# Loading the first MLP weight in four pieces of 512 columns instead of six, with the column blocks of chunk 0 reordered to match

## The chip, the cores and the metric

The kernel runs on one core of a Trainium2 chip. The metric is the device time of one execution in microseconds, the median over several runs; lower is better. Matrix products run on TensorE (PE in the profile; its weight loads are PEld), elementwise work on VectorE (DVE), ScalarE (ACT) and GpSimd (POOL); SyncE (SP) and GpSimd issue the transfers (DMA) that bring inputs from HBM to SBUF.

## What is computed

Linear attention over 8 batches of 8 heads (sequence 576, head size 64), and on its output, seen as 4608 tokens of 512 features, a two-layer MLP with a SiLU between:

```
q_s = softmax of q over the features of a head
k_s = softmax of k over the sequence
kv  = k_s^T v                       # 64 x 64 per head
x   = (q_s kv), heads side by side  # 4608 x 512
h   = x @ w_in                      # 512 -> 2048
out = silu(h) @ w_out               # 2048 -> 512
```

Inputs and output are float32; the kernel works in bfloat16 with float32 sums.

## The kernel before, in words

**Tiling.** The 4608 tokens are cut into 9 chunks of 512 (`NCH`, line 60). All that concerns chunk t and the attention of a later batch is interleaved in stage t by a plan written out by hand: `PLAN[t]` gives for each step a position in the stage, and lines 641 to 731 put all steps in one list, sort it by position and call them. Every engine then runs its own instructions in that order. `STEADY` is the plan of stages 3 to 7. The first product of chunks 0 and 1 and half of that of chunk 2 are plain, as is the second product of chunk 0; all others run by a scheme with seven products in place of eight.

**The start.** Batch 0 is loaded by SP (lines 558 to 562). GpSimd copies one element of v(0) into `gate` (line 583), so that its own loads begin only when the first half of v(0) is there, and then issues the loads of `WORDER` (line 28): the first four at line 584, the rest at line 635. The first weight `w_in`, 512 x 2048, becomes `W1` in bfloat16; `load_w` (line 567) brings it in six pieces: `w10` to `w13` of 256 columns each, `w14` and `w15` of 512. The number is the place in the columns; the order of loading is w11, w13, w10, w12, w14, w15. Behind them on the same queue stand q, k, v of batch 1 and the four pieces of the second weight (`w20` to `w23`, line 575). A float32 source and a bfloat16 destination: a piece of 256 columns writes 256 KB, one of 512 writes 512 KB.

**Chunk 0.** Its first product runs over 16 blocks of 128 columns of `w_in`, each in two halves: `part[0]` cuts the first 576 tokens into 320 and 256. `PLAN[0]['order']` lists the 32 block-halves (block, half). `mm1` (line 243) issues the four matmuls of one (line 251) into a PSUM buffer of a ring of six; `act1` (line 260) writes its silu from there into `GT` (line 281), for a 256-wide half in two instructions of 192 and 64, since chunk 0 ends inside it. The first two entries of the order are begun before the attention output `XT` is complete (line 632: the two quarters that are there, the others when the loop comes by). The second product of chunk 0 is `mm2` (line 523, matmuls at line 530).

**Around it.** In the same stage ScalarE takes the exponentials of batch 1 (line 114), between silus, each change with a table load; `vcast` copies v into `vaug` (lines 123 and 125); `kv` (line 171) multiplies k and v into `kvps` (line 178); `kvcopy` (line 186) scales that by the reciprocal of the sums into `kvn`, on VectorE (line 198) or ScalarE (line 196), as the plan's `ke` says for each half `cc`; `xt` (line 203) makes from it the next chunk's input (line 220). In stages 2 to 8 `product1` (line 319) and `sum1` (line 353) form the first product, `silu1` (line 379) its silu, `presum` (line 396) sums over `GT`, on the engine that `pbe` names, and `product` (line 422) the second product.

Of the kernel before, what the change touches and what calls it, by code (L numbers as in the profile page):

```python
# [9 lines left out]
BF16 = mybir.dt.bfloat16  # L10
# [2 lines left out]
AX = mybir.AxisListType  # L13


PLAN = {
    0: {'y': [31.0, 31.5, 33.5, 34.0, 34.0, 34.5, 35.0, 35.5, 36.0, 38.5, 40.0, 41.0, 42.0, 44.0, 45.5, 46.5], 'ex': [28.8, 28.3, 35.8, 30.3], 'qs': [38.0, 36.5], 'qn': [38.51, 38.01], 'vs': [31.5, 39.5], 'ks': [43.0, 40.5], 'kc': [46.01, 43.6], 'lq': 41.5, 'tp': 40.5, 'ox': [47.5, 47.5], 'oc': [47.51, 47.6], 've': [2, 1], 'order': [(3, 0), (2, 0), (0, 0), (0, 1), (3, 1), (5, 0), (6, 0), (4, 0), (2, 1), (1, 0), (7, 1), (1, 1), (11, 1), (8, 1), (6, 1), (12, 0), (11, 0), (14, 0), (10, 1), (4, 1), (12, 1), (7, 0), (8, 0), (5, 1), (13, 0), (10, 0), (9, 1), (13, 1), (15, 1), (9, 0), (15, 0), (14, 1)], 'ke': [1, 0], 'oe': [1, 1], 'qe': [1, 0], 'pad': 16},
    1: {'ex': [15.2, 17.22, 22.74, 19.26], 'qs': [18.0, 18.5], 'qn': [18.01, 19.1], 'vs': [24.0, 20.0], 'ks': [26.0, 22.0], 'kc': [27.01, 26.01], 'lq': 13.5, 'lk': 19.6, 'lv': 22.2, 'tp': 19.5, 'ox': [28.0, 28.0], 'oc': [28.51, 28.51], 've': [2, 2], 'pa': [10.9, 13.5, 14.0], 'pae': [0, 0, 0], 'ke': [0, 0], 'oe': [2, 0], 'std': 4, 'order': [], 'add': {}, 'act': {}, 's1': {0: 1, 1: 0, 2: 0, 3: 1}, 'sl': [2.5, 2.5, 2.0, 6.0, 4.5, 6.0, 6.0, 9.0, 8.0, 9.0, 10.5, 11.0, 12.5, 14.0, 15.0, 15.0], 'xs': [7.3, -20.9, 0.5, -6.5], 'xe': [0, 1, 1, 1], 'pad': 14, 'qe': [1, 0]},
    2: {'std': 2, 'order': [(3, 1), (3, 6), (2, 1), (2, 6), (3, 7), (3, 5), (2, 2), (2, 7), (3, 4), (3, 2), (2, 5), (2, 4), (2, 3), (3, 3)], 'y': [-12.5, -12.5, -11.5, -11.0, -11.0, -10.0, -10.0, -10.0, -9.0, -8.0, -5.5, -2.5, -2.0, -1.0], 'ex': [-1.207, -2.202, -0.08, 1.794], 'qs': [9.4, 3.4], 'qn': [11.41, 6.91], 'vs': [1.42, 11.4], 'ks': [19.4, 19.4], 'kc': [19.41, 19.41], 'lq': 19.95, 'lk': 14.762, 'lv': 26.91, 'tp': 12.9, 'ox': [19.9, 20.4], 'oc': [19.91, 20.91], 'sl': [4.5, 5.0, 2.5, 7.5, 5.0, 6.0, 10.0, 10.5], 'add': {(3, 6): 10.55, (3, 7): 12.55, (3, 3): 22.02, (3, 2): 16.02, (3, 1): 9.55, (3, 5): 13.55}, 'act': {(2, 3): 21.02, (3, 5): 17.02, (3, 3): 22.02, (2, 5): 18.55, (3, 4): 18.55, (2, 2): 18.02, (3, 1): 10.02, (2, 1): 11.55, (2, 6): 12.02, (3, 2): 17.55, (2, 4): 21.02}, 's1': {2: 0, 3: 1}, 'xs': [0.1, 1.1, 8.1, 8.1], 'pa': [19.45, 20.45, 20.95], 'ya': {5: -6.0, 3: 1.0, 4: -2.05}, 'm1': [0, 0], 'pb': [-14.4, -13.8, -13.9, -15.5, -9.5], 'xe': [0, 0, 0, 0], 'pae': [1, 1, 1], 'pbe': [0, 0, 0, 1, 0], 've': [1, 2], 'ke': [0, 1], 'oe': [1, 0], 'qe': [1, 0]},
}  # L20
STEADY = {'std': 0, 'order': [(0, 1), (0, 6), (0, 5), (0, 7), (0, 2), (1, 1), (0, 4), (1, 6), (0, 3), (2, 1), (1, 2), (1, 7), (1, 5), (2, 6), (1, 4), (1, 3), (2, 2), (2, 7), (2, 5), (2, 4), (3, 1), (3, 6), (2, 3), (3, 2), (3, 7), (3, 5), (3, 4), (3, 3)], 'y': [0.5, 1.5, 5.0, 6.0, 9.0, 9.5, 9.5, 12.5, 14.5, 18.0, 19.5, 22.5, 25.7, 28.402], 'ex': [3.798, 1.41, 3.92, 1.297], 'qs': [11.4, 6.9], 'qn': [12.41, 9.91], 'vs': [10.9, 12.92], 'ks': [19.4, 19.4], 'kc': [21.91, 20.41], 'lq': 8.95, 'lk': 23.9, 'lv': 24.41, 'tp': 17.4, 'ox': [23.4, 23.4], 'oc': [24.41, 26.41], 'sl': [], 'add': {(3, 6): 22.02, (0, 3): 8.02, (0, 2): 6.02, (0, 5): 5.02, (2, 2): 20.02, (1, 3): 15.55, (1, 4): 15.55, (2, 7): 17.55, (1, 2): 10.55, (0, 4): 8.02, (1, 1): 6.02, (2, 6): 14.55, (1, 6): 10.55, (3, 1): 20.55, (1, 7): 11.55, (3, 2): 24.02}, 'act': {(0, 2): 4.55, (0, 3): 10.02, (2, 5): 18.55, (0, 4): 9.02, (1, 5): 15.02, (3, 3): 27.404, (1, 3): 18.02, (0, 5): 5.02, (3, 4): 26.55, (1, 4): 17.02, (2, 4): 23.02, (2, 3): 23.02, (0, 6): 4.02, (1, 1): 8.02, (3, 6): 22.55, (0, 1): 2.55, (3, 5): 27.55, (2, 1): 13.02, (3, 2): 23.55, (3, 7): 27.02, (1, 7): 13.55, (2, 6): 15.02, (2, 7): 17.02, (1, 2): 12.55}, 's1': {0: 0, 1: 1, 2: 0, 3: 0}, 'xs': [0.296, 0.298, -0.227, 0.4], 'pa': [19.95, 27.407, 27.41], 'pb': [1.45, 1.96, 4.45, 5.46, 3.45], 'ya': {6: 8.0, 5: 18.5, 4: 22.95, 3: 28.852, 7: 14.5}, 'm1': [0, 0], 'xe': [0, 0, 1, 1], 'pae': [1, 1, 1], 'pbe': [0, 0, 1, 1, 1], 've': [1, 2], 'ke': [0, 1], 'oe': [0, 0], 'qe': [1, 1]}
for _t in range(3, 8):
    PLAN[_t] = STEADY
PLAN[8] = {'std': 0, 'order': [(0, 1), (0, 6), (0, 2), (0, 7), (1, 1), (0, 5), (0, 4), (0, 3), (1, 6), (1, 2), (1, 7), (1, 5), (1, 4), (2, 1), (1, 3), (2, 6), (2, 2), (2, 7), (2, 5), (3, 1), (2, 4), (2, 3), (3, 6), (3, 2), (3, 7), (3, 5), (3, 4), (3, 3)], 'y': [1.5, 2.0, 5.5, 8.5, 10.0, 11.0, 14.0, 15.0, 19.5, 22.0, 24.5, 25.8, 27.401, 27.406], 'sl': [], 'add': {(2, 7): 17.55, (3, 2): 24.02, (3, 7): 24.55, (3, 4): 26.55, (3, 1): 20.55, (2, 3): 22.55, (0, 2): 3.55, (0, 3): 8.02, (2, 4): 20.55, (1, 4): 14.02}, 'act': {(2, 1): 15.55, (3, 6): 24.02, (3, 4): 26.55, (2, 3): 24.55, (2, 4): 21.55, (1, 7): 14.02, (2, 6): 19.02, (0, 3): 10.02, (1, 5): 12.55, (0, 4): 8.02, (3, 5): 27.403, (1, 4): 15.02, (2, 7): 21.02, (3, 7): 25.55, (1, 6): 10.02, (1, 3): 15.55, (3, 2): 23.55, (2, 2): 19.02, (3, 1): 20.02, (0, 5): 7.55, (1, 1): 6.55}, 's1': {0: 1, 1: 0, 2: 1, 3: 1}, 'xs': [-0.71, -0.208, -0.207, 1.4], 'pa': [24.45, 27.45, 29.429], 'pb': [0.793, 3.96, 10.45, 8.46, 9.45], 'ya': {6: 10.0, 4: 27.401, 7: 15.45, 2: 11.95}, 'm1': [0, 0], 'xe': [0, 0, 1, 0], 'pae': [1, 1, 1], 'pbe': [0, 1, 0, 1, 0]}
PLAN[9] = {'y': [0, 1, 2, 3, 4, 5, 6, 7, 8, 9, 10, 11, 12, 13], 'ya': {}, 'm1': [0, 0], 'pb': [-0.201, -0.2, -0.2, 1.9, 2.9], 'pbe': [0, 0, 0, 0, 0]}
TXAT = [(0, (0, -10.0, 0, 0)), (0, (0, 16.0, 1, 0)), (1, (1, -24.5, 0, 1)), (1, (0, 20.5, 1, 0)), (2, (0, 25.5, 0, 1)), (2, (2, -28.0, 1, 0)), (3, (2, -25.0, 0, 0)), (3, (1, -12.5, 1, 0))]
TWAT = [(1, -7.0, 1), (0, 38.0, 0), (1, 3.5, 0), (0, 46.0, 0), (1, 9.5, 1), (1, 20.5, 0), (1, 10.0, 0), (0, 39.0, 0)]
WORDER = ['w11', 'w13', 'w10', 'w12', 'w14', 'w15', 'q', 'w21', 'w20', 'k', 'w22', 'v', 'w23']
GATE = ('vt', 0)
HV = (1, 0.0, 0)  # L30
JS = 5
STD = 0
START = {'qn': (0, 0), 'h': [3, 3, 2, 2], 'v': 0, 't': (0, 0, 0, 2), 'x': 1, 'o': 0, 'w': 4}

@with_exitstack
def kernel(
# [13 lines left out]
    nc = tc.nc  # L50
# [6 lines left out]
    NC = DM // 128  # L57
# [10 lines left out]
    glob = ctx.enter_context(tc.tile_pool(name="glob", bufs=1))  # L68
# [15 lines left out]
    warm = glob.tile([128, 512], BF16, name="warm")  # L84
    dummy = glob.tile([1, 1], FP32, name="dummy")
    gate = glob.tile([1, 8], FP32, name="gate")

    ld = ctx.enter_context(tc.tile_pool(name="ld", bufs=1))
    ap = ctx.enter_context(tc.tile_pool(name="ap", bufs=2))
# [5 lines left out]
    st = [dict() for _ in range(B)]  # L95
# [13 lines left out]
    def exp(b, src, dst, cc, js=(0, J)):  # L109
        if dst not in st[b]:  # L110
            st[b][dst] = ap.tile([128, J, NG * D], BF16, name=dst, bufs=1)
        js = slice(*js)
        o = st[b][dst][:, js, cc * 128:(cc + 1) * 128].rearrange("p j (g d) -> p j g d", d=D)
        nc.scalar.activation(out=o, in_=jgd(st[b][src], cc)[:, js], func=ACT.Exp)  # L114

    def vcast(b, cc, eng, gs=(0, 2)):
        if gs[0] == gs[1]:
            return
        gs = slice(2 * cc + gs[0], 2 * cc + gs[1])
        o = vaug.rearrange("p j (g e) -> p j g e", e=E1)[:, :, gs, 0:D]  # L120
        i = st[b]["vt"][:, gs, :].rearrange("p g (j d) -> p j g d", d=D)
        if eng is nc.scalar:
            eng.copy(out=o, in_=i)
        else:
            eng.tensor_copy(o, i)
# [167 lines left out]
    def xsum(t, i):  # L293
        V = ENG[PLAN[t]["xe"][i]]
        w = width(t)
# [57 lines left out]
    def sum1(t, g, k):  # L353
# [12 lines left out]
        if k == 1:  # L366
            if PLAN[t]["s1"][g]:
                nc.vector.tensor_scalar_mul(out=new("s1"), in0=o, scalar1=1.0)
# [182 lines left out]
    PSB = {"ring": 6, "ops": 2}  # L551


    nc.vector.memset(dummy, 0.0)
    nc.vector.memset(warm, 0.0)
    nc.scalar.activation(out=dummy, in_=dummy, func=ACT.Exp)
# [9 lines left out]

    def load_w(name):
        if name[:2] == "w1":
            f = slice(*((0, 256), (256, 512), (512, 768), (768, 1024), (1024, 1536), (1536, 2048))[int(name[2])])
            nc.gpsimd.dma_start(  # L570
                out=W1[:, :, f], in_=w_in[:, f].rearrange("(c p) f -> p c f", p=128)
            )
        elif name[:2] == "w2":
            i = int(name[2])
            nc.gpsimd.dma_start(
                out=W2[:, i * 4:(i + 1) * 4, :],
                in_=w_out[i * 512:(i + 1) * 512, :].rearrange("(fc p) o -> p fc o", p=128),
            )
        else:
            load(1, name + "t", {"q": q, "k": k, "v": v}[name], eng=nc.gpsimd)  # L580

    gx = st[0][GATE[0]]
    nc.gpsimd.tensor_copy(gate[:, 0:1], gx[0:1, 2 * GATE[1] + 1, 0:1])
    for name in WORDER[:START["w"]]:
        load_w(name)

    wps = ps.tile([128, 512], FP32, name="wps", tag="ops", bufs=PSB["ops"])

# [7 lines left out]
    for cc in range(2):  # L596
        exp(0, "qt", "eq", cc)
        qsum(0, cc)
        if cc == 0 or not SB["o"]:
            qnorm(0, cc, ENG[SB["qn"][cc]])  # L600
    exp(0, "kt", "ek", 0)
    vcast(0, 0, nc.scalar)
    exp(0, "kt", "ek", 1)
    for js in HALF:
# [77 lines left out]
    for t in range(NCH):  # L682
        p = PLAN[t]
# [4 lines left out]
        else:  # L688
# [4 lines left out]
            for i, (g, m) in enumerate(p["order"]):  # L693
                x = i + 4 * p["std"]
# [9 lines left out]
    for t in range(1, NCH):  # L704
        for i, (m, a) in enumerate(HALVES):
            x = PLAN[t + 1]["y"][i]
# [14 lines left out]
    for t in range(1, NCH):  # L721
# [5 lines left out]
        for i in range(5):  # L727
            n, h = ((0, 1), (1, 1), (2, 1), (3, 0), (3, 1))[i]
# [33 lines left out]
```

## Time and profile before

| | |
|---|---|
| median of 6 runs | 273.05 us (271.61 to 274.58) |
| the profiled execution | 272.63 us |
| span of its profile | 270.8 us |
| granted TensorE clock | 1.0 throughout |
| HBM read, written | 36.70 MB, 9.44 MB |

The profile is of one execution, and times in it count from the start of the span. Its page gives the busy time of each engine, the transfers, the chain of work that ended last, and groups of instructions; behind it stands the trace, which can be asked for the timeline of a stretch, for the waits of an engine, or for one line of the kernel. A group reads: line, engine, operation, tile written <- tile read, count. `W<-in_moe_w_in_dram` is a load of `w_in`, `hps` the PSUM tile of the first product, `ops` that of the second. The time of a load counts from its issue on GpSimd's queue to its landing.

### The profile page before, as it was taken

What the parts mean: (1) busy time and instruction counts of PE and PEld (TensorE: products, weight loads), DVE (VectorE), ACT (ScalarE), POOL (GpSimd) and SP (SyncE); (2) the same over time, 40 slices, a digit from 0 to 9 for tenths busy, and PEclk for the clock granted to TensorE, in tenths of its full rate; (3) what the DMA queues carried; (4) which work ended last, traced back from release to release, by engine and by line L of the source; (5) the groups of instructions that cost most, each with busy time, mean ns of one, the idle gap of its engine ahead of it and who ended that gap; (6) DMA issues with size and microseconds to landing.
All of it is one profiled execution on the core that took longest, in us unless ns stands there. A gap on an engine that the chain in (4) does not pass through costs nothing.

```text
span 270.8 us, 6537 instructions
## 1 busy us (share of the span) xinstructions
PE 254.2 (94%) x2668; PEld 198.5 (73%) x2668; DVE 199.6 (74%) x343; ACT 190.3 (70%) x317; POOL 145.0 (54%) x91
## 2 busy tenths in 40 slices
PE   8769999998998899999999999999999999999992
PEld 3437844456764778888888888887888887888882
DVE  2933476845968977978996899688978678898832
ACT  5678999578749897977987798769875457444300
POOL 1577126213302869794979397849685546604500
PEclk9999999999999999999999999999999999999999
DMA  7999998980797795579745965482531102110324
GB/s 255 307 164 292 273 317 157 363 315 0 222 289 257 95 346 187 192 139 309 238 127 119 325 238 117 102 306 94 119 84 45 40 21 59 41 39 18 78 65 116
DMA packets 44014, 46.50 MB, mean 172 GB/s; under 512 B 18640, under 2 KB 31952, under 8 KB 43984
## 3 DMA queue, kind: packets, MB, share of 16 engines
q1 hardware_dynamic: 37728, 38.22, 47.8%
q0 software_dynamic: 6096, 7.73, 13.4%
q8 instruction: 21, 0.34, 0.5%
q10 hardware_dynamic: 160, 0.13, 0.2%
q14 instruction: 9, 0.07, 0.1%
HBM read 36.70 MB, written 9.44 MB: 170 GB/s over the span
## 4 chain that ended last, share of the span: by engine, by line
PE 53%; DMA 14%; ACT 10%; DVE 10%; issue 5%; POOL 4%; SPq 2%; DVEq 0%; POOLq 0%; ACTq 0%
PE ops L445 22%; PE hps L344 20%; PE hps L251 9%; DMA kt<-in_k_dram 5%; DMA qt<-in_q_dram 4%; DMA W<-in_moe_w_in_dram 3%; DVE u L362 3%; DVE zq L133 2%; DMA qT<-eq 2%; ACT GT L281 2%; ACT eq L114 2%; ACT L114 2%; ACT ek L114 2%; ACT L281 1%; POOL eq L141 1%
## 5 line engine op out<-in xcount | busy, mean ns | idle before, releaser
L445 PEld LDWEIGHTS <-GT 128*128 128x128 bf16 x512 | 49.5, 98 | 8.0 <-issue 1.8
L344 PEld LDWEIGHTS <-TX 128*128 128x128 bf16 x416 | 40.2, 98 | 8.5 <-issue 3.2
L344 PE MATMUL hps<-XS,TX 128*128 128x256 bf16 x312 | 43.3, 273 | 1.8 <-DVE u L362 0.9
L362 DVE SCALAR_TENSOR_TENSOR u<-hps,u 128x512 f32<-128x512 f32 x52 | 35.8, 688 | 8.9 <-PE hps L344 6.1
L362 DVE SCALAR_TENSOR_TENSOR u<-hps,s 128x512 f32<-128x512 f32 x52 | 35.5, 683 | 9.2 <-PE hps L344 9.0
L445 PEld LDWEIGHTS <-SW 128*128 128x128 bf16 x384 | 37.3, 98 | 5.4 <-DVE SW L402 1.0
L251 PE MATMUL hps<-XT,W 128*128 128x320 bf16 (+3 forms) x224 | 36.0, 318 | 3.3 <-DMA W<-in_moe_w_in_dram 1.8
L386 ACT ACTIVATE GT<-u 128x512 bf16<-128x512 f32 x52 | 32.2, 630 | 9.9 <-DVE u L362 9.9
L251 PEld LDWEIGHTS <-W 128*128 128x128 bf16 x224 | 21.6, 98 | 17.3 <-issue 2.9
L406 POOL TENSOR_TENSOR SW<-GT,SW 128x1024 bf16<-128x1024 bf16 x12 | 26.1, 2171 | 14.7 <-DVE SW L402 14.7
L344 PEld LDWEIGHTS <-W 128*128 128x128 bf16 x312 | 30.4, 98 | 4.0 <-issue 0.2
L445 PE MATMUL ops<-TW,SW 128*128 128x256 bf16 x256 | 32.8, 273 | 0.5 <-DVE SW L402 0.5
L445 PE MATMUL ops<-TW,GT 128*128 128x256 bf16 x256 | 32.7, 273 | 0.3 <-DVE u L467 0.3
L445 PE MATMUL ops<-W,GT 128*128 128x256 bf16 x256 | 31.7, 272 | 0.7 <-ACT s L475 0.5
L141 POOL TENSOR_TENSOR eq<-eq,rzq 128x1152 bf16<-128x1152 bf16 x11 | 23.5, 2140 | 15.9 <-DVE rzq L134 10.8
L133 DVE TENSOR_REDUCE zq<-eq 128x18 f32<-128x1152 bf16 x16 | 21.5, 1342 | 13.2 <-ACT eq L114 13.2
L344 PE MATMUL hps<-XT,W 128*128 128x256 bf16 x208 | 30.4, 273 | 0.0
L281 ACT ACTIVATE GT<-hps 128x192 bf16<-128x192 f32 (+4 forms) x72 | 26.0, 408 | 5.8 <-PE hps L251 4.4
L400 POOL TENSOR_TENSOR SW<-GT 128x1024 bf16<-128x1024 bf16 x7 | 14.9, 2129 | 27.7 <-ACT GT L386 17.6
L404 POOL TENSOR_TENSOR GT<-GT 128x1024 bf16<-128x1024 bf16 x12 | 25.5, 2127 | 0.0
L114 ACT ACTIVATE eq<-qt 128x1152 bf16<-128x1152 f32 x16 | 18.3, 1156 | 8.6 <-DMA qT<-eq 4.5
L386 ACT ACTIVATE GT<-s 128x512 bf16<-128x512 f32 x26 | 16.4, 630 | 10.0 <-DVE s L362 10.0
(79 smaller groups left out, 392.8 us busy)
## 6 DMA issues: line engine op xcount, KB each, us to landing
qt<-in_q_dram SPq DMA_DIRECT2D x6, 1152.0 KB, 5.8
kt<-in_k_dram SPq DMA_DIRECT2D x6, 1152.0 KB, 6.1
vt<-in_v_dram SPq DMA_DIRECT2D x6, 1152.0 KB, 9.0
out_dram<-u SPq DMA_DIRECT2D x34, 64.0 KB, 3.2
W<-in_moe_w_out_dram POOLq DMA_DIRECT2D x4, 512.0 KB, 18.2
out_dram<-u SPq DMA_DIRECT2D x14, 128.0 KB, 2.5
qt<-in_q_dram SPq DMA_DIRECT2D x2, 576.0 KB, 4.1
kt<-in_k_dram SPq DMA_DIRECT2D x2, 576.0 KB, 7.7
```

What stands on the lines that cost most here:

```text
L114: nc.scalar.activation(out=o, in_=jgd(st[b][src], cc)[:, js], func=ACT.Exp)
L133: nc.vector.reduce_sum(out=st[b]["zq"][:, cc, js], in_=e, axis=AX.X)
L141: eng.tensor_tensor(out=e, in0=e, in1=r[:, :, :, None].to_broadcast([128, n, 2, D]), op=ALU.mult)
L251: nc.tensor.matmul(out=hps[:, 0:size], lhsT=W1[:, c, fb * 128:(fb + 1) * 128], rhs=XT[t][:, c, off:off + size], start=(c == 0), stop=(c == ...
L281: nc.scalar.activation(out=y, in_=hps[:, h], func=ACT.Silu)
L344: nc.tensor.matmul(out=o[:, f, :], lhsT=l(c, 2 * g + f), rhs=r(c), start=bool(first and f == 0 and c == 0), stop=(c == HK - 1), skip_group ...
L362: nc.vector.scalar_tensor_tensor(out=out, in0=o, scalar=1.0, in1=x, op0=ALU.mult, op1=ALU.add)
L386: nc.scalar.activation(out=y, in_=MP[t, g, x], func=ACT.Silu)
L400: V.tensor_add(S1[:, f], quad(t, 0, f, 1), quad(t, 1, f, 1))
L404: V.tensor_sub(quad(t, 0, f, 1), quad(t, 0, f, 0), quad(t, 0, f, 1))
L406: V.tensor_sub(S4[:, f], quad(t, 1, f, 0), S2[:, f])
L445: nc.tensor.matmul(out=o, lhsT=l(f), rhs=r(f), start=bool(first and (own or a == 0) and f == 0), stop=(f == HF - 1), skip_group_check=True,)
```

## The change

The first weight comes in four pieces of 512 columns (blocks 0 to 3, 4 to 7, 8 to 11, 12 to 15), in that order, three of them issued at the gate and the fourth behind. The 32 block-halves of chunk 0 are put in an order that uses up one piece before the next; the first five stay as they were. The gate and the first loads move down in the program, behind the exponentials of batch 0, without a change of their place among GpSimd's instructions. In the steady plan `ke` sends the kv copies of half 0 to ScalarE as well, and one presum has another position; in stage 8 three presums, one product, one sum and one silu have. `WARM` is 0, and nothing under it is built.

```diff
+WCUT = ((0, 512), (512, 1024), (1024, 1536), (1536, 2048))
+WARM = 0
 PLAN[0]:
-'order': [(3, 0), (2, 0), (0, 0), (0, 1), (3, 1), (5, 0), (6, 0), (4, 0), (2, 1), (1, 0), (7, 1), (1, 1), (11, 1), (8, 1), (6, 1), (12, 0), (11, 0), (14, 0), (10, 1), (4, 1), (12, 1), (7, 0), (8, 0), (5, 1), (13, 0), (10, 0), (9, 1), (13, 1), (15, 1), (9, 0), (15, 0), (14, 1)]
+'order': [(3, 0), (2, 0), (0, 0), (0, 1), (3, 1), (2, 1), (1, 0), (1, 1), (5, 0), (6, 0), (4, 0), (7, 1), (6, 1), (4, 1), (7, 0), (5, 1), (11, 1), (8, 1), (11, 0), (10, 1), (8, 0), (10, 0), (9, 1), (9, 0), (12, 0), (14, 0), (12, 1), (13, 0), (13, 1), (15, 1), (15, 0), (14, 1)]
 STEADY:
-'pb': [1.45, 1.96, 4.45, 5.46, 3.45], ... 'ke': [0, 1]
+'pb': [1.45, 1.96, 4.45, 4.46, 3.45], ... 'ke': [1, 1]
 PLAN[8]:
-'y': [..., 15.0, 19.5, 22.0, ...], 'add': {..., (1, 4): 14.02}, 'pb': [0.793, 3.96, 10.45, 8.46, 9.45]
+'y': [..., 15.0, 19.0, 22.0, ...], 'add': {..., (1, 4): 13.55}, 'act': {..., (2, 5): 20.02}, 'pb': [0.793, 3.96, 12.45, 10.46, 11.45]
-WORDER = ['w11', 'w13', 'w10', 'w12', 'w14', 'w15', 'q', 'w21', 'w20', 'k', 'w22', 'v', 'w23']
+WORDER = ['w10', 'w11', 'w12', 'w13', 'q', 'w21', 'w20', 'k', 'w22', 'v', 'w23']
-START = {..., 'w': 4}
+START = {..., 'w': 3}
     def load_w(name):
         if name[:2] == "w1":
-            f = slice(*((0, 256), (256, 512), (512, 768), (768, 1024), (1024, 1536), (1536, 2048))[int(name[2])])
+            f = slice(*WCUT[int(name[2])])
-    gx = st[0][GATE[0]]
-    nc.gpsimd.tensor_copy(gate[:, 0:1], gx[0:1, 2 * GATE[1] + 1, 0:1])
-    for name in WORDER[:START["w"]]:
-        load_w(name)
...
     exp(0, "kt", "ek", 0)
+    gx = st[0][GATE[0]]
+    gx = gx[0:1, 2 * GATE[1] + 1, 0:1] if GATE[0][1] == "t" else gx[0:1, 0, GATE[1] * 128:GATE[1] * 128 + 1]
+    nc.gpsimd.tensor_copy(gate[:, 0:1], gx)
+    for name in WORDER[:START["w"]]:
+        load_w(name)
     vcast(0, 0, nc.scalar)
```

## The prediction

> **What bounds the kernel now.** First the page: one engine is nearly full, TensorE, so only time in which it stands still or starts late can be won.
>
> ```profile
> PE 254.2 (94%) x2668; PEld 198.5 (73%) x2668; DVE 199.6 (74%) x343; ACT 190.3 (70%) x317; POOL 145.0 (54%) x91
> ```
>
> Then the waits, of TensorE alone (us in total, times, longest). One wait for a transfer stands first; the rest of the list is under 1.3 us each.
>
> ```profile
> PE hps L251 <- DMA W<-in_moe_w_in_dram: 1.8, 1, 1.8
> ...
> PE kvps L178 <- ACT ek L114: 0.6, 1, 0.6
> ```
>
> Then the timeline around it (start, duration, instruction, idle time before).
>
> ```profile
> 10.13 4.65 POOL L570 DMA_DIRECT2D W<-in_moe_w_in_dram  x6
> ...
> 15.89 0.82 DVE L236 CAST XT<-o 128x320 bf16<-128x320 f32 x2 [0.51 <-PE o L220]
> ...
> 15.90 1.26 PE L251 MATMUL hps<-XT,W 128*128 128x320 bf16 x8
> ...
> 16.65 1.28 ACT L281 ACT_TABLE_LOAD   x1
> ...
> 18.99 15.00 PE L251 MATMUL hps<-XT,W 128*128 128x320 bf16 x120 [1.83 <-DMA W<-in_moe_w_in_dram]
> ```
>
> Chunk 0 is 128 matmuls. The first 8 (blocks 3 and 2) end at 17.16; then TensorE idles 1.83 us for the piece that holds block 0, and the other 120 run without a gap. The line of the loads, asked for one issue at a time, gives issue to landing in the order w11, w13, w10, w12, w14, w15:
>
> ```profile
> DMA to landing us min/median/max: 4.0/4.0/4.0
> ...
> DMA to landing us min/median/max: 6.5/6.5/6.5
> ...
> DMA to landing us min/median/max: 7.1/7.1/7.1
> ...
> DMA to landing us min/median/max: 7.7/7.7/7.7
> ...
> DMA to landing us min/median/max: 9.5/9.5/9.5
> ...
> DMA to landing us min/median/max: 11.4/11.4/11.4
> ```
>
> With the issue starts 10.13, 11.07, 11.80, 12.54, 13.27 and 14.00 the pieces land at 14.1, 17.6, 18.9, 20.2, 22.8 and 25.4. Third place in the queue is what block 0 waits for. Two rates can be read: after the first landing, 3 pieces of 256 KB take 6.1 us (126 KB/us); the two of 512 KB take 5.2 us (197 KB/us).
>
> Last the chain of waits behind chunk 0, and the timeline there. ScalarE carries the chain from 31 to 46 us; GpSimd's cast of v(1) starts when that load lands, and TensorE's kvps follows at once.
>
> ```profile
> 31.20 1.75 ACT GT L281 x7
> ...
> 45.14 1.17 ACT ek L114
> ...
> 46.36 0.48 PE kvps L178 x36
> ```
> ```profile
> 41.73 1.64 POOL L125 CAST vaug<-vt 128x1152 bf16<-128x1152 f32 x1 [0.59 <-DMA vt<-in_v_dram]
> ...
> 43.42 0.48 PE L178 MATMUL kvps<-vaug,ek 64*64 64x65 bf16 x36
> ```
>
> **The change, part by part.**
>
> *The first piece.* Four pieces of 512 columns in the order of use; w10 holds blocks 0 to 3, so the wait before block 0 goes, and the first matmul of all waits for twice the bytes; behind that matmul stand all of chunk 0 on TensorE and ScalarE's first silu. When does w10 land? The first 256 KB landed at 14.1. Lower end: another 256 KB at the best rate, 256/197 = 1.3, so 15.4. Upper end: the same bytes as the first two pieces land when the second did, 17.6. I take the rate that the queue showed in just this stretch, 256/126 = 2.0, so 16.1: the row nearest in time, though of smaller pieces. The activations are no earlier anyway: VectorE's copies into XT end at 15.89 + 0.82 = 16.71, and half of the first 8 matmuls need them; and ScalarE's table load ends at 16.65 + 1.28 = 17.93. With w10 at 16.1 the first 8 end at about 17.25 and the 120 follow: start 17.25 for 18.99, a gain of 1.7. In general the gain is 17.93 less the landing (18.99 less the 8 matmuls' 1.06 in a run at 0.133 each), at most 1.83.
>
> The trace shows 126 KB/us for pieces of 256 columns and 197 for those of 512. The Trainium skill, "DMA: Bandwidth & Descriptors", section "Specifications", has transfers at line rate from 512 bytes up; a row of 256 bf16 columns is just that, so by the rule wider pieces move bytes no faster, w10 lands at 17.6, the gain is 0.3 and the time 272.3, against 271.1 by the rows. The two rates above speak against the rule, but they are also of different moments of one queue.
>
> *The later pieces.* In the new order block-halves 9, 17 and 25 are the first to need w11, w12 and w13. At 15.00/120 x 4 = 0.5 us each, TensorE comes to them at about 20.2, 24.2 and 28.2. From 16.1 at 2.6 us per 512 KB they land at 18.7, 21.3 and 23.9. No wait; even the landings of before (20.2, 22.8, 25.4) would do. The same activations are written, in other places: one 256-wide half goes behind the exponentials in place of a 320-wide one, 0.45 for 0.385, +0.07 on ScalarE there. ScalarE has 29 block-halves before its table load at 32.97: 15 x 0.385 + 14 x 0.45 to 0.49 = 12.1 to 12.6 us, from 17.95 to 30.1 to 30.6; TensorE's pace ends them at about 31.1 to 31.3. It follows TensorE, but closely; I take off 0.1.
>
> *The queue behind.* GpSimd issues four loads of W1, not six, 0.75 us each: 1.5 us less, and a load waits for the landing of the eighth before it (the issue of k at 18.11 after w13's landing at 17.6, w_out's at 19.23 after 18.9, v's at 20.91 after 20.2). So k goes out without that wait, v after w11, the last piece of w_out after w12; none is later. The bytes end at 23.9 for 25.4, so all behind them, q, w_out, k and v, lands about 1.5 earlier. This matters for v: 41.6 becomes 40.1, the cast ends at about 41.85, kvps can run at 41.9 for 43.42. That is the tightest joint, and it caps the gain at 1.5. The weight sums on VectorE and GpSimd (L317) come earlier too, and nothing waits for them.
>
> *The kv copies.* In stages 3 to 6 the two scalings of column half 0 go from VectorE to ScalarE: 4 x 0.48 = 1.9 us less there, 4 x 0.52 = 2.1 more here.
>
> ```profile
> 169.28 0.48 DVE L198 TENSOR_SCALAR kvn<-kvps,rz 128x64 bf16<-128x64 f32 x2
> 171.03 0.69 DVE L362 SCALAR_TENSOR_TENSOR u<-hps,u 128x512 f32<-128x512 f32 x1 [1.27 <-PE hps L344]
> ```
> ```profile
> 170.21 0.60 ACT L370 ACTIVATE s<-hps 128x512 f32<-128x512 f32 x1 [0.55 <-PE hps L344]
> 170.71 0.62 ACT L386 ACTIVATE GT<-s 128x512 bf16<-128x512 f32 x1
> 171.75 0.63 ACT L386 ACTIVATE GT<-u 128x512 bf16<-128x512 f32 x1 [0.42 <-DVE u L362]
> ```
>
> VectorE gains nothing: it then waits 1.27 for TensorE. On ScalarE the pair stands behind the copy of line 370, from 170.7 to 171.2; TensorE reads kvn at 172.23, 1.0 us later, and the two silus behind run into an idle of 0.42. Nought, between -0.1 and +0.5 a stage should that cover be gone.
>
> *Stage 8 and the rest.* Two sums over GT on VectorE (L406, L404) go behind three evictions. L404 then ends at about 240.6, and TensorE's product that reads it starts at 240.75; TensorE shows no wait after 229.4. Nought, between 0 and +0.3. The smaller numbers of the plan (a presum's place in the steady stages, one product's) move no instruction on any queue; one pair of silus changes places. SP's queue is unchanged. After 50 us TensorE's waits are 0.3 to 0.9 each and none is on a load of the weights, and the loads of later batches are issued behind work that moves with it; so I let a start gained stay gained.
>
> *Sum.* Profiled execution: 272.63, span 270.8 and 1.8 around it. Less min(1.7 - 0.1, 1.5) = 1.5: 271.1. The shown median is 0.42 above that execution, which gives 271.6. I name 271.3, between them.
>
> **The rivals.**
>
> *B, larger rows move no faster:* w10 lands at 17.6, gain 0.3, 272.3. For it: the second piece's 3.5 us after the first has no cause in the trace, and it may come at that time whatever the size. Against: 197 KB/us as soon as 512-column pieces run.
>
> *C, the gain is given back before kvps:* v(1) lands no earlier, kvps stays at 43.42, and only TensorE's 0.61 us before 46.36 is won back: 272.0. For it: the cast waited 0.59 for v. Against: everything ahead of v in the queue ends earlier.
>
> *D, slower:* the first piece lands late, after 17.93, from which point TensorE starts later than before. A piece is there when its slowest share is; if both halves of w10 take what the second piece took, 3.5 each from 14.1 - 2.0 = 12.1, it lands at 19.1: 1.2 lost, 273.8. At w12's landing of before, 20.2, it is 2.3 lost, 274.9. Against: the first piece in fact took 2.0 in that reckoning.
>
> **How the numbers follow.** A, as summed: 0.55, its own range 270.0 to 272.4. B 0.20, C 0.10, D 0.15. Eight in ten: from 269.7 (A at 1.83, with the 1 to 1.5 by which the runs shown differ from their median) to 274.0 (the nearer half of D). One per cent, 2.7 us, is about what a measurement of this kernel can tell from no change. Faster by more needs A's most and a good draw: a quarter of A, 0.14. Slower by more is the worse half of D: 0.07. The rest, 0.79, is within 1%.
>
> **What would show it.** Right: no wait of TensorE for W between its first and last matmul of chunk 0; first landing 15.4 to 16.5 with intervals near 2.6; the 128 matmuls ending near 32.4; kvps of 43.42 at about 41.9; the last product 1.5 earlier. Wrong: a first L251 matmul after 17 (B, D); kvps still at 43.4 (C); a TensorE wait on kvn in stages 3 to 6 or at L445 near 239 (the parts taken at nought).

## The result and the profile after

| | before | after |
|---|---|---|
| median | 273.07 us (82 runs, 270.34 to 277.69) | 270.56 us (40 runs, 268.87 to 274.07) |
| profiled execution, span | 272.63, 270.8 us | 269.95, 268.0 us |

After to before is 0.9919, with a 95% interval of 0.9902 to 0.9935: 2.2 us faster, 1.8 to 2.7 by the interval. The forecast was 271.3 within 269.7 to 274.0, by a gain of 1.5. The ratio, like every mean below, leaves out the executions that took over 1.5% longer than the fastest of their kernel.

Line numbers of the kernel after are higher: `mm1`'s matmuls 255 for 251, `mm2`'s 534 for 530, `kv`'s 182 for 178, the loads 578 and 583 for 570 and 575. First the page; the engines are as full as before.

```profile
PE 254.2 (95%) x2668; PEld 198.8 (74%) x2668; DVE 197.4 (74%) x335; ACT 191.3 (71%) x325; POOL 143.1 (53%) x89
```

TensorE's waits of after (us in total, times, longest). The load of `w_in` that stood at the top with 1.8 is gone; a load of `w_out` is in the list for the first time.

```profile
...
PE hps L348 <- DVE XS L305: 1.0, 2, 0.5
...
PE ops L534 <- DMA W<-in_moe_w_out_dram: 0.8, 1, 0.8
```

TensorE's timeline of after:

```profile
15.63 15.85 PE L255 MATMUL hps<-XT,W 128*128 128x320 bf16 x128
32.27 9.66 PE L534 MATMUL ops<-W,GT 128*128 128x512 bf16 x44 [0.79 <-DMA W<-in_moe_w_out_dram]
41.92 0.48 PE L182 MATMUL kvps<-vaug,ek 64*64 64x65 bf16 x36
42.33 1.90 PE L534 MATMUL ops<-W,GT 128*128 128x512 bf16 x8
44.28 0.48 PE L182 MATMUL kvps<-vaug,ek 64*64 64x65 bf16 x36
...
48.84 3.34 PE L255 MATMUL hps<-XT,W 128*128 128x448 bf16 x16 [0.52 <-DVE XT L240]
```

The 128 matmuls of chunk 0 now run as one group to 31.48. Then TensorE stands 0.79 us for `w20`. The second `kvps`, which waited 0.61 for `ek` before, has no wait and follows the eight products ahead of it. The same two places in before's timeline:

```profile
46.36 0.48 PE L178 MATMUL kvps<-vaug,ek 64*64 64x65 bf16 x36 [0.61 <-ACT ek L114]
...
50.90 1.26 PE L251 MATMUL hps<-XT,W 128*128 128x448 bf16 x5 [0.52 <-DVE XT L236]
```

So the lead over before, in the two profiled executions, runs like this:

| | before | after | lead |
|---|---|---|---|
| first load of `w_in` issued | 10.13 | 9.86 | 0.27 |
| first matmul of chunk 0 | 15.90 | 15.63 | 0.27 |
| its second product | 33.83 | 32.27 | 1.56 |
| `kvps` | 43.42 | 41.92 | 1.50 |
| `kvps`, second | 46.36 | 44.28 | 2.08 |
| first product of stage 1 | 50.90 | 48.84 | 2.06 |

The first 0.27 is there before the change can have moved a wait: the issue follows v(0)'s landing, which differs between executions. In the profiled executions that have this gate it lay between 9.45 and 9.94 with the changed start of the program and between 9.63 and 10.18 with before's; whether the change has a part in that is not shown. From 48.84 on the lead grows to 2.8 by the last products; that differs between executions (below).

The loads of `w_in` in after, one issue each (for a window with two issues the largest number belongs to the later one):

```profile
DMA to landing us min/median/max: 5.6/5.6/5.6
...
DMA to landing us min/median/max: 5.6/6.8/7.9
...
DMA to landing us min/median/max: 7.9/8.7/9.6
...
DMA to landing us min/median/max: 9.6/10.5/11.4
```

With issues at 9.86, 10.80, 11.53 and 12.27 the pieces land at 15.5, 18.7, 21.1 and 23.6. The chain of waits of after, taken between 9 and 52 us, leaves chunk 0 early and waits for one load, that of v(1):

```profile
19.39 21.19 DMA vt<-in_v_dram
...
40.60 1.17 ACT vaug L127
...
43.07 1.17 ACT ek L118
...
44.28 0.48 PE kvps L182 x36
```

From 19.4 to 40.6 us what ends last is GpSimd's queue of loads; from there it is ScalarE, which casts its half of v, loads a table, takes `ek`, and lets the second `kvps` go. In before the load of v(1), issued at 20.91, has this line, and ScalarE's timeline shows the same two steps:

```profile
DMA to landing us min/median/max: 20.7/20.7/20.7
```
```profile
42.68 1.16 ACT L123 CAST vaug<-vt 128x1152 bf16<-128x1152 f32 x1
...
45.14 1.16 ACT L114 ACTIVATE ek<-kt 128x1152 bf16<-128x1152 f32 x1
```

and of after:

```profile
40.60 1.17 ACT L127 CAST vaug<-vt 128x1152 bf16<-128x1152 f32 x1 [0.21 <-DMA vt<-in_v_dram]
...
43.07 1.16 ACT L118 ACTIVATE ek<-kt 128x1152 bf16<-128x1152 f32 x1
```

In before ScalarE came to the cast 1.08 us after v had landed (41.60) and waited for nothing: its own work, the silus of chunk 0, was late. In after it is there 0.21 before v lands.

### The profile page after: what moved, and what is told of

Same layout as the page of the kernel before. It is cut to its first block, busy times and chain, and to the rows that moved or that the text cites. A ratio compares the mean times of both kernels' runs of the same rounds, so it can differ in the third digit from the quotient of the medians.

```text
span 268.0 us, 6534 instructions
## 1 busy us (share of the span) xinstructions
PE 254.2 (95%) x2668; PEld 198.8 (74%) x2668; DVE 197.4 (74%) x335; ACT 191.3 (71%) x325; POOL 143.1 (53%) x89
## 4 chain that ended last, share of the span: by engine, by line
PE 58%; DMA 19%; DVE 9%; ACT 6%; SPq 3%; issue 2%; DVEq 0%; ACTq 0%
PE ops L449 24%; PE hps L348 23%; DMA vt<-in_v_dram 11%; DMA kt<-in_k_dram 7%; PE hps L255 6%; DVE u L366 2%; DVE zq L137 2%; PE kvps L182 2%; PE o L224 1%; ACT eq L118 1%; ACT ek L118 1%; DVE s L366 1%; SPq L523 1%; SPq L155 1%; PE ops L534 1%
## 5 line engine op out<-in xcount | busy, mean ns | idle before, releaser
L366 DVE SCALAR_TENSOR_TENSOR u<-hps,u 128x512 f32<-128x512 f32 x52 | 35.8, 688 | 10.6 <-PE hps L348 8.4
L410 POOL TENSOR_TENSOR SW<-GT,SW 128x1024 bf16<-128x1024 bf16 x12 | 26.0, 2170 | 14.7 <-DVE SW L406 14.7
L404 POOL TENSOR_TENSOR SW<-GT 128x1024 bf16<-128x1024 bf16 x7 | 14.9, 2127 | 27.5 <-ACT GT L390 16.9
L285 ACT ACTIVATE GT<-hps 128x64 bf16<-128x64 f32 (+4 forms) x72 | 25.3, 419 | 4.3 <-PE hps L255 3.0
```

The costliest lines, as they stand in the source:

```text
L285: nc.scalar.activation(out=y, in_=hps[:, h], func=ACT.Silu)
L366: nc.vector.scalar_tensor_tensor(out=out, in0=o, scalar=1.0, in1=x, op0=ALU.mult, op1=ALU.add)
L404: V.tensor_add(S1[:, f], quad(t, 0, f, 1), quad(t, 1, f, 1))
L410: V.tensor_sub(S4[:, f], quad(t, 1, f, 0), S2[:, f])
```

## The experiments

Each ratio is to before on the same chip, with its 95% interval; the runs come from three chips, called the first to the third here. The standard error of a mean is 0.2 to 0.4 us for 9 to 12 executions, and 0.2 for before, of which each chip has 27 to 29. Before's mean was 272.70 on the first chip, 272.54 on the second and 271.93 on the third.

### Which part of the change: the start or the plan

`start_only` has the pieces, the two orders and the count at the gate; the steady plan and stage 8 are before's. `plan_only` is the reverse.

```diff
 plan_only, against before:
-STEADY 'pb': [..., 5.46, 3.45], 'ke': [0, 1]
+STEADY 'pb': [..., 4.46, 3.45], 'ke': [1, 1]
 (and PLAN[8] as in the change)
```

> The change without its edits to the plans of stages 3 to 8: pieces, loading order and the order of chunk 0 alone. Theory (all of the gain is made before 50 us, by the shorter load of W1): the same time as the changed kernel, 0.992 of before, the kvps that stood at 46.36 us at about 44.3, the last product about 2.7 us earlier than before. Rival (the plan edits carry the part that appears after 50 us, 2.07 growing to 2.76): about 0.7 us less gain, 0.9945.

> The kernel before with only the edits to the plans of stages 3 to 8 (kv copies of half 0 on ScalarE, the sums of stage 8 moved). Theory: nought, 1.000 within 0.002, as VectorE waits for TensorE behind the copies. Rival: 0.7 us faster, 0.9975, with the gain between 100 and 190 us.

Measured: `start_only` 270.66, 0.9908 (0.9866 to 0.995); `plan_only` 273.02, 1.001 (0.997 to 1.0049). The gain is in the start. The kv copies on ScalarE and stage 8, taken at nought, show none, though the interval of `plan_only` leaves room for 0.8 us less or 1.3 more.

What of the lead that grows past 50 us? From the beginning of stage 1 to the end of the span the six profiles with before's plan of stages 3 to 8 take 218.9 to 221.1 us (mean 220.1; before 219.9, `start_only` 220.4), the eight with the changed plan 218.6 to 220.1 (mean 219.2; after 219.2). The 0.7 by which after's lead grows is within the scatter of either group. Part of the scatter has a name, the transfers `qT<-eq`. TensorE waits for them like this in `start_only` and then in after:

```profile
PE o L224 <- DMA qT<-eq: 1.6, 3, 1.0
```
```profile
PE o L224 <- DMA qT<-eq: 0.4, 1, 0.4
```

It is 1.5 in `before_again` and 1.8 in `six_again`. The three that waited long all have before's plan; whether the plan has a part in that is open.

### The order or the width

`six_in_landing_order` keeps before's six pieces and their order of loading and changes only the order in which chunk 0 uses them. It ran on the first chip beside `start_only`; `six_again` is the same kernel, run on the third chip beside `after_again`, the changed kernel once more. `eight_256`, on the second chip, is the changed kernel with all of `w_in` in pieces of 256 columns.

```diff
 six_in_landing_order, against before: only
 PLAN[0]['order']: blocks in the order in which w11, w13, w10, w12, w14, w15 land
 eight_256, against after:
-WCUT = ((0, 512), (512, 1024), (1024, 1536), (1536, 2048))
+WCUT = tuple((256 * i, 256 * i + 256) for i in range(8))
-START = {..., 'w': 3}
+START = {..., 'w': 6}
```

> The kernel before, six pieces as they were, only the block-halves of chunk 0 put in the order in which those pieces land (blocks 2, 3, then 6, 7, then 0, 1, then 4, 5). Theory (the pieces' size counts, because the queue behind them ends earlier): the wait of 1.83 us in chunk 0 goes, but the first matmul of the second layer then waits for its weight at about 33.2 us and kvps stays near 43.4, so at most 0.6 us is left, 0.998. Rival (only the wait in chunk 0 counted): all of it stays, 0.993.

> The changed kernel with all of the first weight in eight pieces of 256 columns, loaded in the same order: the suspected cost of small rows doubled against the six pieces of before. Theory (rows of 512 bytes move more slowly): the last piece lands 15.5 to 17 us after the first issue instead of 13.8 to 14.2, v(1) 1 to 2 us later than in the changed kernel, the time 1 to 2 us above it, 0.996 to 1.000 of before. Rival (rows of 512 bytes are at line rate): landings within 0.5 us of the changed kernel's, 0.992.

> The changed kernel once more, for the granted clock of each execution and for the second landing. Theory: first landing 5.5 to 5.9 after its issue, the later ones 2.4 to 3.2 apart; ratio 0.990 to 0.9935; at most 1 in 10 executions with a mean clock of 0.994 or less, and with those left out on both sides a gain of 1.5 us, 1.2 to 1.8, which is the wait. Rival (the gain is mostly the clock): with those left out the gain is under 0.7 us.

> The six pieces of before in the same order of loading, with chunk 0 in the order of their landing, once more, beside the changed kernel on the same chip. Theory: the order removes the wait, the wider pieces bring the loads behind about 1 us forward (v at 40.6 for 41.6), of which little reaches the end: 0.9925 to 0.9955, the changed kernel 0.5 to 0.8 us faster. Rival (the width does nothing that lasts): the same ratio as the changed kernel within 0.2 us.

Measured: `six_in_landing_order` 271.44, 0.9941 (0.9906 to 0.9976), nearer to its rival than to its theory. That looked as if the order did most. The repeat said otherwise: `six_again` 271.90, 0.999 (0.9957 to 1.0023), beside `after_again` 270.50, 0.9947 (0.9915 to 0.998); both gained less than expected. `eight_256`: 272.55, 0.9991 (0.9953 to 1.0028), the time expected, though its last piece landed 14.7 us after the first issue and not 15.5 or more. By means on the same chip, the changed start is faster than six pieces in landing order by 0.9 (270.71 and 271.61) and 1.2 us (270.64 and 271.84); the order alone is worth 1.1 (272.70 and 271.61) and 0.1 (271.93 and 271.84). Each of the four differences has a standard error of 0.4 to 0.5. Together they give about 1.1 for the pieces and 0.6 for the order; which is larger is not shown. The 1.0 between the two readings of the order lies mostly in before, which was 0.8 faster on the third chip; six pieces in landing order took 271.61 and 271.84.

The pieces differ in more than width. With more of them v(1) is also issued later (20.91 in before, 22.59 in `eight_256`, 19.39 in after), and `eight_256` begins chunk 0 at 16.35, after a wait of 0.58, since its first block lies in the second piece. No run separates the width of the pieces from their number.

How far two executions of one kernel can be apart shows in the two profiles of six pieces in landing order; the one profiled first was among the faster of its run (270.84), the other was the slowest (273.61). TensorE's timeline of `six_in_landing_order`:

```profile
15.46 15.85 PE L251 MATMUL hps<-XT,W 128*128 128x320 bf16 x128
32.55 9.66 PE L530 MATMUL ops<-W,GT 128*128 128x512 bf16 x43 [1.23 <-DMA W<-in_moe_w_out_dram]
42.22 0.48 PE L178 MATMUL kvps<-vaug,ek 64*64 64x65 bf16 x36
```

and of `six_again`:

```profile
15.83 2.13 PE L251 MATMUL hps<-XT,W 128*128 128x320 bf16 x16
19.76 13.89 PE L251 MATMUL hps<-XT,W 128*128 128x320 bf16 x112 [1.79 <-DMA W<-in_moe_w_in_dram]
35.15 9.66 PE L530 MATMUL ops<-W,GT 128*128 128x512 bf16 x44 [1.50 <-DMA W<-in_moe_w_out_dram]
44.74 0.48 PE L178 MATMUL kvps<-vaug,ek 64*64 64x65 bf16 x36
```

In the second the wait for W is back, at another block, and the load of `w20` is later too: the second piece landed at 19.71, 5.7 us after the first. The landings of `w_in` and of v(1) in all profiled executions, from the loads' own lines, with the beginning of stage 1's first product (`gate_k` and `first_split` follow below):

| kernel | first issue | first landing | second | last of `w_in` | v(1) | stage 1 |
|---|---|---|---|---|---|---|
| before | 10.13 | 14.10 | 17.56 | 25.39 | 41.60 | 50.90 |
| `plan_only` | 10.02 | 13.99 | 17.68 | 25.46 | 41.69 | 52.40 |
| `before_again` | 10.18 | 14.14 | 17.69 | 26.50 | 42.72 | 53.32 |
| `before_heat` | 10.04 | 14.05 | 16.36 | 25.45 | 41.71 | 50.96 |
| `six_in_landing_order` | 9.63 | 13.77 | 15.73 | 24.21 | 40.88 | 49.13 |
| `six_again` | 10.06 | 14.03 | 19.71 | 27.19 | 43.39 | 51.64 |
| `eight_256` | 9.93 | 14.26 | 16.31 | 24.61 | 41.81 | 50.07 |
| after | 9.86 | 15.48 | 18.73 | 23.64 | 40.58 | 48.84 |
| `start_only` | 9.75 | 15.32 | 19.00 | 23.95 | 40.91 | 49.16 |
| `after_again` | 9.45 | 15.26 | 18.66 | 23.52 | 40.27 | 48.52 |
| `w20_first` | 9.62 | 15.30 | 18.72 | 23.74 | 40.25 | 48.50 |
| `w20_kv` | 9.94 | 15.80 | 19.19 | 24.22 | 40.53 | 48.82 |
| `first_split` | 9.67 | 13.63 | 16.63 | 24.28 | 40.71 | 49.56 |
| `gate_k` | 8.53 | 15.48 | 18.61 | 23.53 | 39.80 | 48.67 |

With six pieces all of `w_in` is there 14.6 to 17.1 us after the first issue, with four and the same gate 13.8 to 14.3. The largest part of the spread is the second piece of 256 columns, 2.0 to 5.7 us behind the first; the other 256-column pieces follow in 1.0 to 2.6. With four pieces the second lands 3.1 to 3.7 behind the first each time. What holds the second small piece is open. Behind it the width makes no difference that these profiles show: the last four pieces of `eight_256` land 1.2 to 1.4 us apart, the last two of after 2.4 and 2.6 with twice the bytes.

The last two columns are the plainest reading of what the change moves. In after, `start_only`, `after_again`, `w20_first`, `eight_256` and both runs of six pieces in landing order stage 1 begins 8.25 us after v(1) lands: the chain that starts with ScalarE's cast. (`w20_kv` has 8.29, by another path: there VectorE casts, and TensorE waits for `w23`.) In before and `before_heat` it is 9.3, in `first_split` and `gate_k` (below) 8.9: there ScalarE comes to the cast late. With the half clock, in `plan_only` and `before_again`, it is 10.7 and 10.6.

### The first piece in two

`first_split` is the changed kernel with its first piece as two of 256 columns.

```diff
-WCUT = ((0, 512), (512, 1024), (1024, 1536), (1536, 2048))
+WCUT = ((0, 256), (256, 512), (512, 1024), (1024, 1536), (1536, 2048))
-START = {..., 'w': 3}
+START = {..., 'w': 4}
```

> The changed kernel with its first piece of 512 columns loaded as two of 256. Theory (rows of 512 bytes move more slowly than rows of 1024): the second half lands at 16.1 to 17.6 us instead of 15.5, the later pieces and v(1) 0.5 to 1 us later than in the changed kernel, the time 0.3 to 1 us above it, about 0.995 of before. Rival (rows of 512 bytes are at line rate): landings and time as in the changed kernel, 0.992.

Measured: 271.14, 0.9935 (0.9901 to 0.997), so no better than after; the mean, 270.87 beside `start_only`'s 270.71 on the same chip, is not surely worse either. TensorE's timeline of `first_split`:

```profile
16.68 15.85 PE L255 MATMUL hps<-XT,W 128*128 128x320 bf16 x128 [1.17 <-DMA W<-in_moe_w_in_dram]
```

The first half lands at 13.63, the second at 16.63, and chunk 0 begins with the second. That is 7.0 us from the first issue; the same 512 columns in one piece took 5.6 to 5.9. v(1), at 40.71, is only 0.1 later than in after. Chunk 0 ended at 32.5 and TensorE's wait for `w20` had no place left, so only part of the delay came through.

### What TensorE hangs on from 31 to 43 us

`w20_first` swaps the loads of `w21` and `w20`, so that the wait of 0.79 should go. `w20_kv` also moves the first of the two `kvps` later in stage 0, so that TensorE has other work while v lands, and gives ScalarE's cast of v to VectorE.

```diff
 w20_first, against after:
-WORDER = ['w10', 'w11', 'w12', 'w13', 'q', 'w21', 'w20', 'k', 'w22', 'v', 'w23']
+WORDER = ['w10', 'w11', 'w12', 'w13', 'q', 'w20', 'w21', 'k', 'w22', 'v', 'w23']
 w20_kv, besides:
-PLAN[0] 'vs': [31.5, 39.5], 'ks': [43.0, 40.5], 've': [2, 1]
+PLAN[0] 'vs': [38.9, 39.5], 'ks': [43.0, 42.5], 've': [0, 1]
```

> The changed kernel with the first two pieces of the second weight swapped, so that the one that its first matmuls need comes 2.5 us sooner. Theory (two waits in a row: this one of 0.8 us, then kvps for v(1) near 41.9): the first wait goes, and nearly all of it comes back before kvps, so the time stays within 0.3 us of the changed kernel's, 0.991. Rival (that wait is what caps the gain): 0.8 us faster than the changed kernel, 0.988.

> The kernel of the swap, and besides both kv products of batch 1 put behind two more groups of the second layer (TensorE has work while v(1) lands) and the cast of the other half of v(1) moved from ScalarE to VectorE, so that the last exponential does not stand behind it. Theory: TensorE passes both waits, stage 1's first product starts 0.8 to 1.2 us earlier than in the changed kernel, and that reaches the end, 0.987. Rival (the casts of v(1) on VectorE and GpSimd at once hold each other up, or the copies behind kvps come late): no gain on the changed kernel, 0.991 or worse.

Measured: `w20_first` 271.50, 0.9958 (0.9928 to 0.9988); `w20_kv` 271.02, 0.9957 (0.9928 to 0.9986). By the ratios neither is better than after (0.9919 and, repeated, 0.9947), and the 0.987 that `w20_kv` was to reach is refuted; the changed kernel itself was not run on this chip. TensorE's timeline of `w20_first`:

```profile
31.28 9.66 PE L534 MATMUL ops<-W,GT 128*128 128x512 bf16 x44
41.59 0.48 PE L182 MATMUL kvps<-vaug,ek 64*64 64x65 bf16 x36 [0.65 <-POOL vaug L129]
```

and of `w20_kv`:

```profile
31.54 10.52 PE L534 MATMUL ops<-W,GT 128*128 128x512 bf16 x48
42.96 1.02 PE L534 MATMUL ops<-W,GT 128*128 128x512 bf16 x4 [0.91 <-DMA W<-in_moe_w_out_dram]
```

The wait changes its place and keeps its size: 0.79 at `w20`, then 0.65 at v(1), then 0.91 at `w23`, the last load of the queue (landed at 42.92). Counted from the first issue, stage 1 begins 38.98 later in after, 38.88 in both of these.

`gate_k` lets GpSimd's loads begin with the first half of k(0) in place of v(0).

```diff
-GATE = ('vt', 0)
+GATE = ('kt', 0)
```

> The changed kernel with GpSimd's loads held back until the first half of k(0) is there, not of v(0): the queue of loads begins at about 8.3 in place of 9.9, 1.5 us earlier, and competes with the two halves of v(0) and the second half of k(0). Theory (from chunk 0's end to 43 us TensorE hangs on this queue at three places, w20, v(1) and the last piece of w_out): all that is loaded lands 1.0 to 1.5 us earlier, the wait of 0.8 for w20 goes, kvps at 40.5 to 41, and as batch 0's v comes later, by 0.5 to 1, chunk 0 starts 0.3 to 0.8 later: 0 to 0.8 us faster than the changed kernel, ratio to before 0.988 to 0.992. Rival (the batch 0 inputs bound the start): v(0) lands 1.5 or more later, chunk 0 starts 1 us or more later, and the kernel is 0.5 to 1 us slower than the changed one, ratio 0.994 to 0.996.

Measured: 269.91, 0.9925 (0.9896 to 0.9954), beside `after_again`'s 0.9947 (0.9915 to 0.998) on the same chip. The means are 269.97 and 270.64, with standard errors of 0.22 and 0.30, so 0.7 with an error of 0.4: the best median of all kernels here, but not surely better than the change. Its first load of `w_in`:

```profile
DMA to landing us min/median/max: 7.0/7.0/7.0
```

The first piece was issued 1.3 us earlier than in after, at 8.53, and landed at the same 15.48 (7.0 for 5.6): the expected 1.0 to 1.5 did not come for `w_in`, whose last piece landed at 23.53 for 23.64. v(1) came at 39.80, 0.5 to 0.8 earlier than in after and `after_again`, and `w20` at 31.45, in time for TensorE. ScalarE then took over:

```profile
31.49 9.66 PE L534 MATMUL ops<-W,GT 128*128 128x512 bf16 x44
41.17 0.48 PE L182 MATMUL kvps<-vaug,ek 64*64 64x65 bf16 x36
...
44.12 0.48 PE L182 MATMUL kvps<-vaug,ek 64*64 64x65 bf16 x36 [0.63 <-ACT ek L118]
```

The second `kvps` waits for `ek` again, as in before, and stage 1 begins at 48.67, between the two profiles of the changed kernel.

### The clock after the wait

The profile of `plan_only`, whose start is before's, showed a granted clock of one half in chunk 0. `before_again` is before without any edit, one execution, to see whether that recurs.

> The kernel before, unchanged, for a second profile. Open is whether the 3.5 us between the landings of its first two pieces are of the kernel or of the execution: theory (of the kernel: small rows while GpSimd still issues) 3 us or more again; rival (of the execution) 2 us or less.

Measured: 276.31 us for that one execution, and the half clock again. Its second piece landed 3.5 us behind its first, as in before; but `before_heat` (2.3) and `six_in_landing_order` (2.0) load the same pieces in the same order, so that time is of the execution. Stretches of 1 us (busy TensorE, weight loads, VectorE, ScalarE, GpSimd, then the granted clock) of `before_again`:

```profile
19.00:20.00 1.00, 0.00 (x0) 0.00 (x0) 0.00 (x0) 0.00 (x0) 0.00 (x0) 0.83 1.34 202
20.00:21.00 1.00, 0.69 (x3) 0.43 (x4) 0.00 (x0) 0.00 (x0) 0.45 (x1) 0.50 1.26 206
...
23.00:24.00 1.00, 1.00 (x9) 0.70 (x7) 0.00 (x0) 0.63 (x3) 0.00 (x0) 0.96 1.27 256
```

The wait for W was 3.09 us here, 2.00 in `plan_only`, 1.83 in before and 1.79 in `six_again`; the clock fell to 0.50 after the first two and stayed at 1.00 after the others. The 120 matmuls of `plan_only` then ran from 19.06 to 35.33, where TensorE took up the next product; in before 18.99 to 33.83. So the half clock costs 1.4 us in this stage, and 1.1 in `before_again` (20.31 to 36.24). Was it part of the change's gain? `before_heat` keeps TensorE busy in the wait.

```diff
+    put(0, 1.5, heat, 8)
     for _, _, f, args in sorted(todo, key=lambda x: x[:2]):
```

> The kernel before, with eight products into a scratch PSUM tile (0.21 us each, 1.7 us) put on TensorE between the first 8 matmuls of chunk 0 and the others: the wait for w10 stays, but TensorE is busy in most of it. The output is the reference's; the eight products are not used. Clock theory (in some executions the idle time at this wait halves the granted clock for 3.4 us, which costs about 2 us; the rest of what the change gains, 1.5, is the wait itself): the 120 matmuls still begin at 18.9 to 19.4, executions with a mean granted clock of 0.994 or less become rare (14 of 73 with the old order so far, 2 of 33 with the new pieces and order), and the mean over all executions falls by 0.2 to 0.4, ratio 0.9985 to 0.9993; no half clock between 19 and 24 us. Rival 1 (the low clock has to do with other things than this wait): the share of such executions stays near 1 in 5, ratio 1.000 or, where eight products last longer than the wait, 1.001 to 1.002. Rival 2 (the low clock is nearly all of the change's gain): ratio 0.993 to 0.995.

Measured: 271.51, 0.9999 (0.9961 to 1.0036). TensorE's timeline of `before_heat`:

```profile
16.91 1.89 PE L591 MATMUL wps<-warm 128*128 128x512 bf16 x8
18.64 6.44 PE L251 MATMUL hps<-XT,W 128*128 128x320 bf16 x52
25.49 8.56 PE L251 MATMUL hps<-XT,W 128*128 128x320 bf16 x68 [0.41 <-DMA W<-in_moe_w_in_dram]
```

Here `w10` was there at 17.73, before the eight products ended, so this profile shows no wait for it. A half clock of 3.4 us in 270 lowers the mean clock by 0.006, so an execution that had one is among those at 0.994 or less; here that is one of 12. A low mean alone does not say where the clock was low: after's 0.995 comes from its last 5 us, behind the last matmul (263.14), where the clock was 0.76 on average. Filling the wait does not speed the kernel up, which speaks against the rival that the clock is nearly all of the gain; but the filling itself can hide a part, since here TensorE went on only 0.9 us after `w10` was there. Whether it makes the low clock rarer, 12 executions cannot tell. A second count decides more: of the executions compared, 10 of 84 of before (on the three chips) and 3 of 38 of after (from the result) have such a clock. With them the means are 272.38 and 270.45, without them 272.24 and 270.34. The gain is 1.9 us either way; counted over every execution, 19 of 96 and 6 of 41, it is 2.0 either way, and beside `start_only` alone 2.4 with and 1.9 without. So the clock is at most a small part of the gain.

## Why the prediction held, and where it was off

**The first piece: right.** Landing 15.48, between the lower end of 15.4 and the 16.1 taken. Counted from the first issue it came 1.65 us later than before's first piece, where the sum had 2.0. But the rate behind that 2.0, 126 KB/us for pieces of 256 columns, was misread. Of the three pieces that it averages, the second came 3.46 us after the first, the other two 1.38 and 1.30 after one another: 185 to 197 KB/us, as for 512 columns. That the landing fell inside the named bounds is in part luck: the 2.0 is the mean of one piece that was held up and two that were not.

**Rival B, larger rows no faster: refuted in what it forecast.** The first piece landed at 15.26 to 15.80 in five executions, not at 17.6. The Trainium skill, "DMA: Bandwidth & Descriptors", section "Specifications", puts line rate from 512 bytes up. In the running queue this case agrees: `eight_256`'s last four pieces land 1.2 to 1.4 us apart, those of twice the size in before and after 2.4 to 2.6. What failed is the step from there to a landing at 17.6, since the second small piece's delay is not a matter of rate. In all `eight_256` took 14.7 us from its first issue to the last landing of `w_in`, four pieces 13.8 to 14.3; what the six small pieces cost beyond that is mostly the late second one.

**Chunk 0: right.** No wait for W, and the later pieces (18.7, 21.1, 23.6) came in time, the first of them 3.2 us behind the one before it in place of 2.6. The chunk ended 0.9 earlier than named (31.5 for 32.4), which could not be used: the 0.79 at `w20` took most of it back. The forecast said that none behind would be late and did not look at what TensorE needs next after chunk 0.

**v(1) and kvps: the right number by two errors.** `kvps` came at 41.92, forecast 41.9. But v(1) landed at 40.58, not 40.1: 1.02 earlier than in before and 0.75 counted from the first issue, for a forecast of 1.5. `w_in` itself was through 1.5 sooner after its first issue, as forecast (13.8 for 15.3); the loads behind it took 16.9 us in after (23.64 to 40.58) for 16.2 in before, and why is open. GpSimd's cast made up for it, 1.16 us for 1.64. And TensorE itself, with its new wait, came to `kvps` only then; in `w20_first`, without that wait, it stands 0.65 for the cast of v. So the cap was real, and two things stood at it.

**The step that failed: "it caps the gain at 1.5".** The cap was put at the first `kvps`, where v's landing holds TensorE, and carried to the end. But the chain into stage 1 goes over ScalarE, as the prediction itself had read from the profile, and there before had a lag of its own: 1.08 from v's landing to ScalarE's cast, with TensorE's wait of 0.61 for `ek` behind it. That lag went too. On this chain the gain is the 1.02 by which v landed earlier and the 1.08: 2.1, less 0.02 from landing to cast in after; stage 1 begins 2.06 earlier, and 1.8 earlier counted from the first issue. Rival C had priced the 0.61, and the forecast left it out. With these in place of 1.5 the sum ends at 270.6 or 270.8. It is the profiles that show this step. The times alone hardly tell 1.5 from 2: the ratios put the gain at 2.2 (1.8 to 2.7) in the result, 2.5 (1.4 to 3.7) for `start_only` and 1.4 (0.5 to 2.3) for `after_again`. What the lead gains past 50 us, 0.7 here, is within the scatter between profiles; of the 1.5 by which `start_only`'s profiled execution ended later than after's (271.44 for 269.95) 1.2 is its longer wait for `qT<-eq`.

**Rival C, the gain given back before kvps:** half seen. Not v but `w20` gave back 0.8; without it the queue would have taken 0.65 at the next place. **Rival D, a late first piece:** not seen in five executions of four pieces; `first_split` shows the mechanism, a second landing of 16.63 that delays all of chunk 0, short of the 17.93 where it starts to cost.

**The parts taken at nought** showed nothing in `plan_only`, to within about 1 us.

## What to carry to other kernels

When a wait goes, follow the chain past the first cap, on every engine that it passes, and follow the same queue to the next thing it brings: here one new wait of 0.8 came up at once and an old lag of 1.1 left. When TensorE waits on a load queue in several places in a row, reordering the loads or their users only moves the wait; what counts is when the queue's bytes are through. Here four wide pieces were through 13.8 to 14.3 us after their first issue in five executions, five to eight pieces with narrow ones among them 14.6 to 17.1 in eight. One set of runs can credit the wrong part: the order alone was worth 1.1 us in one and 0.1 in the next, mostly because the kernel that it was compared with was 0.8 faster on the other chip. And a rate that is an average over one late transfer and two prompt ones is no rate: read the landings one by one.

## What the hardware showed that was not expected

Behind a wait of 2.0 us TensorE's clock fell to half, though TensorE worked for part of the 3.4 us before the fall:

```profile
17.00:18.00 1.00, 0.06 (x1) 0.00 (x0) 0.00 (x0) 0.99 (x2) 0.00 (x0) 1.00 1.27 163
18.00:19.00 1.00, 0.00 (x0) 0.00 (x0) 0.00 (x0) 0.60 (x2) 0.76 (x1) 1.00 1.31 191
19.00:20.00 1.00, 0.94 (x4) 0.58 (x5) 0.00 (x0) 0.00 (x0) 0.70 (x1) 0.54 1.26 206
20.00:21.00 1.00, 1.00 (x7) 0.65 (x5) 0.00 (x0) 0.44 (x1) 0.04 (x1) 0.50 1.23 203
...
22.00:23.00 1.00, 1.00 (x8) 0.63 (x6) 0.00 (x0) 0.55 (x3) 0.00 (x0) 0.75 1.23 207
```

These are 1 us stretches of `plan_only`; its first 8 matmuls end at 17.06; the 0.54 and the 0.75 put the fall at 19.08 and the return at 22.5. The Trainium skill, "TensorE: Matmul & The Clock Gate", part 1 on the HAM clock gate, says that the clock falls to half after at least one idle window of about 3.4 us, and that the windows run free of the kernel. The 3.4 us of half clock agree with the window; the idle time does not, since 3.4 us with some 1.4 us of work in them were enough. Why 1.83 and 1.79 us were not is not settled; no run here moves the window by itself.

A load issued earlier need not land earlier: in the profile of `gate_k` the first piece was issued 1.3 us sooner and landed at the same 15.48, in company with the loads of batch 0. There the queue's start was not what its first landing hung on; what it did hang on is open.
